# A partition order (t, part) for stages two and three, so that a chunk of z is one load and a chunk of u one store

## The chip, the cores and the metric

The kernel runs on one core of one Trainium2 chip. Its time is device microseconds of that core, from the launch to the end of the program. The time before is 1523.6 us, the median of 6 runs that lie between 1521.41 and 1527.71.

## What is computed

The reference has two blocks, one after the other. All of it is in float32.

```python
# attention block: a filter in the frequency domain; x is (8, 2496, 256)
X = np.fft.rfft(x, axis=1)
Y = X * (filt_r + 1j * filt_i)[None, :, :]
y = np.fft.irfft(Y, n=2496, axis=1)

# mixture of experts on the 8 * 2496 = 19968 rows; 8 experts, 256 -> 1024 -> 256
logits = x @ w_gate
expert_idx = np.argmax(logits, axis=1)
gate_w = softmax(logits)[arange, expert_idx]
# every row goes through its own expert alone
y = gate_w[:, None] * (np.maximum(x @ w1[expert_idx], 0.0) @ w2[expert_idx])
```

## The kernel before, in words

**The transform.** 2496 is 39 times 64, and the two factors have no common divisor, so the transform of a batch's 2496 rows is done as one of length 39 and one of length 64, with matrices and without twiddle factors in between. As the input is real, the transform of length 39 is kept as 20 frequencies f (`NF`) with two parts each, real and imaginary; the parts are called `c` in the code. The index in the transform of length 64 is `t`.

- Stage A (`stage_a`): the forward transform of length 39. Three values of `t` are handled by one matmul (117 rows in, 120 rows out). Its result `zo` is stored in the DRAM tensor `zd`, whose shape is (64 t, 40 part and f, 256 channels).
- Stage B (`stage_b`): the forward transform of length 64 for two f at a time, with the matrix `tbs` (128 by 128: 64 t times 2 parts), and then the product with the filter `ht` on VectorE, giving `ys`. Its input is a chunk of four f, read from `zd` by `load_z` into a buffer of the tag "in".
- Stage C (`stage_c`): the inverse transform of length 64 with `tcs`, giving `uo`, which is stored in the DRAM tensor `ud` (same shape as `zd`), a chunk of four f at a time.
- Stage D (`stage_d`): the inverse transform of length 39. It reads `ud` by `load_u` as 120 rows by four.

For the first batch there is no way through DRAM: `first_a`, `turn_z`, `first_c` and `turn_u` do the same in the core's memory, with transposes on TensorE from the tiles `zt` and `ut`.

**The partition order.** On the 128 partitions of a chunk of z, and of a chunk of u, the order before is (part, t): the 64 partitions below hold the real part of all t, those above the imaginary part. In `zd` and `ud` the two parts of one t are 20 rows of 256 channels apart. So `load_z` (lines 333 and 334) issues two transfers of 64 partitions, and `stage_c` (lines 392 and 393) two stores of 64 partitions. Each moves 64 pieces of 4 KB.

**Queues.** All direct transfers are issued by SyncE, in order. `move` puts off a store to the next turn of the planner, when `flush` issues it (so all stores have line 307). Transfers by index, which put the rows in the order of the experts (`scatter`, line 615) and the results in the order of the output (`result`, line 855), are issued by GpSimd. The framework gives SyncE's transfers 8 semaphores in turn: a transfer is issued when the one that was issued 8 places earlier has landed.

**Buffers.** Chunks of x, z and u that are read share 7 buffers of 512 KB (tag "in"). `zo` and `uo` share 4 buffers (tag "st"); a copy out of PSUM into one of them waits until its last store has landed.

**What sets the order.** At build time a planner writes down the order of TensorE, VectorE, ScalarE and SyncE. It keeps a model of time (`now`, and `lands` for when a transfer is thought to be there) and mixes the steps of stage A for batch k+1, B and C for batch k, D and the routing for batch k-1, and tiles of the experts' work, for which it asks rows (`rows_in`, tile `xg`) and weights (`weights`, tiles `w1t` and `w2t`). GpSimd's order is not written by hand but comes from the framework's scheduler. From about 950 us on only experts' work is left.

In the changed kernel the four orders written by the planner are the same, instruction by instruction, but that SyncE has one transfer where it had two, at 70 places. GpSimd's order differs at a few places between 155 and 729 us (times of the trace before): the sums of weights (`wsum`, lines 766 to 770) stand ahead of the sums of rows (`sums`, lines 754 to 758) or of one indirect store, where they stood behind or in between.

Of the kernel before, what the change touches and what calls it, by code (L numbers as in the profile page):

```python
# [10 lines left out]
F32 = mybir.dt.float32  # L11
# [8 lines left out]
P = 128  # L20
S = 2496
D = 256
# [5 lines left out]
N2 = 64  # L28
NF = (N1 + 1) // 2
# [6 lines left out]
DH = D // P  # L36
# [5 lines left out]
def token(q, t):  # L42
    return (q * N2 * pow(N2, -1, N1) + t * N1 * pow(N1, -1, N2)) % S


def coefficients():

    k = np.arange(S)
    of = np.zeros((N2, N1), int)
    of[k * pow(N1, -1, N2) % N2, k * pow(N2, -1, N1) % N1] = k  # L50
    return of[:, :NF]


def dft_tables():

    w = 2.0 * np.pi  # L60
    q = np.arange(N1)
    t = np.arange(N2)

    ta = np.zeros((NB, N1, NB, NS))
    td = np.zeros((NB, NS, NB, N1))
    for f in range(NF):
        ang = w * ((q * f) % N1) / N1
        for j in range(NB):
            ta[j, :, j, f] = np.cos(ang)
            td[j, f, j] = (2.0 if f else 1.0) / S * np.cos(ang)  # L70
            if f:
                ta[j, :, j, NF + f] = -np.sin(ang)
                td[j, NF + f, j] = -2.0 / S * np.sin(ang)

    ang = w * ((t[:, None] * t[None, :]) % N2) / N2
    c, sn = np.cos(ang), np.sin(ang)
    tb = np.block([[c, -sn], [sn, c]])
    tc = np.block([[c, sn], [-sn, c]])

    ids = np.zeros((NB, N1, NG))  # L80
    valid = np.zeros((NB, N1, NG))
    for j in range(NB):
        for i in range(len(range(j, N2, NB))):
            ids[j, :, i] = token(q, NB * i + j)
            valid[j, :, i] = 1.0


    sg = np.where(coefficients() <= S // 2, 1.0, -1.0)

    return {  # L90
        "ta": ta.reshape(TP, TK),
        "tb": tb,
        "tc": tc,
        "td": td.reshape(TK, TP),
        "sg": np.concatenate([sg[:, :NF // 2], sg[:, NF // 2:]]),
        "ids": ids.reshape(TP, NG),
        "valid": valid.reshape(TP, NG),
    }
# [22 lines left out]
def kernel(  # L121
# [16 lines left out]
    nc = tc.nc  # L138
    mm = nc.tensor.matmul
# [8 lines left out]
    for b in range(B):  # L148
        GROUPS.append([])
        for rows, most in WANT[b]:  # L150
            n = min(most, max(0, ((b + 1) * S - (N - left) - E * (rows - 1)) // rows))
# [8 lines left out]
    zd = [dram.tile([N2, NS, D], F32, tag=f"z{b % 2}", name="zd") for b in range(B)]  # L160
    ud = [dram.tile([N2, NS, D], F32, tag=f"u{b % 2}", name="ud") for b in range(B)]
# [6 lines left out]
    ident = perm.tile([P, P], F32, name="ident")  # L168
# [38 lines left out]
    pro = first.enter_context(tc.tile_pool(name="pro", bufs=2, side="right"))  # L207
# [7 lines left out]
    def bank():  # L215
        return ps.tile([P, 512], F32, tag="bank", name="bank")
# [5 lines left out]
    def either(n, on_vector, on_scalar):  # L222

        v = max(free["v"], now[0]) + 0.15 + n / 960
        s = max(free["s"], now[0]) + 0.16 + n / 1200
        if v <= s:
            free["v"] = v
            on_vector()
        else:
            free["s"] = s  # L230
            on_scalar()

    def evac(o, i, n):
        either(n, lambda: nc.vector.tensor_copy(o, i), lambda: nc.scalar.copy(out=o, in_=i))
# [6 lines left out]
    HP = P // 2  # L241
# [64 lines left out]
    def move(o, i):  # L306
        moves[1].append(lambda: nc.sync.dma_start(out=o, in_=i))

    def mark(key):
        moves[1].append(lambda: stored.add(key))  # L310
# [7 lines left out]
    def fin(key):  # L318
        ins[key] = sb.tile([P, 4, D], F32, tag="in", name="fin", bufs=NIN)
        return ins[key]  # L320

    def load_x(b, c):
        i0, n = CH[c]
        xt = fin(("x", b, c))

        for j in range(0, n, 2 if (b, c) == (0, 0) else n):
            m = 2 if (b, c) == (0, 0) else n
            nc.sync.dma_start(out=xt[:, j:j + m], in_=x[b, :, i0 + j:i0 + j + m, :])

    def load_z(b, c):  # L330
        f0, n = FH[c]
        zi = fin(("z", b, c))
        nc.sync.dma_start(out=zi[:HP, :n], in_=zd[b][:, f0:f0 + n, :])
        nc.sync.dma_start(out=zi[HP:, :n], in_=zd[b][:, NF + f0:NF + f0 + n, :])

    def load_u(b, c):
        i0, n = CH[c]
# [43 lines left out]
    def stage_c(b, f):  # L381
        ys = outs.pop(("y", b, f))
        j = f % 4
        if j == 0:
            outs["u", b] = sb.tile([P, 4, D], F32, tag="st", name="uo", bufs=4)
        uo = outs["u", b]
        p = bank()
        mm(p, lhsT=tcs, rhs=ys, start=True, stop=True)  # L388
        evac(uo[:, j:j + 2, :], p.rearrange("p (i d) -> p i d", i=2), 512)
        if j == 2:  # L390
            f0 = f - 2
            move(ud[b][:, f0:f0 + 4, :], uo[:HP])
            move(ud[b][:, NF + f0:NF + f0 + 4, :], uo[HP:])
        if f == NF - 2:
            mark(("c", b))

# [19 lines left out]
    zu = {}  # L416

    def first_a(c):
        i0, n = CH[c]
        xt = ins.pop(("x", 0, c))  # L420
        if c == 0:

            zu["z"] = pro.tile([P, DH, NF, 2, N2], F32, name="zt", bufs=1)
            zu["u"] = pro.tile([P, DH, N2, 2, NF], F32, name="ut", bufs=1)
        for j in range(0, n, 2):
            p = bank()[:, :4 * TK]
            for h in range(DH):
                for i in range(2):
                    mm(p[:, (2 * h + i) * TK:(2 * h + i + 1) * TK], lhsT=xt[:TP, j + i, h * P:(h + 1) * P], rhs=tas,
                       start=True, stop=True)  # L430
            t0 = NB * (i0 + j)
            m = min(2 * NB, N2 - t0)
            pv = p.rearrange("p (h t c f) -> p h c f t", h=DH, c=2, f=NF)[:, :, :, :, :m]
            zv = zu["z"].rearrange("p h f c t -> p h c f t")[:, :, :, :, t0:t0 + m]
            for h in range(DH):
                evac(zv[:, h], pv[:, h], 2 * TK)

    def turn_z(f):
        if f % 4 == 0:
            nc.scalar.copy(out=ht[HP:, f:f + 4], in_=ht[:HP, f:f + 4])  # L440
            free["s"] = max(free["s"], now[0]) + 1.1
        zi = outs["zi", f] = pro.tile([P, 2, D], F32, tag="zi", name="zi")
        p = bank().rearrange("p (i h d) -> p i h d", i=2, h=DH)
        for i in range(2):
            for h in range(DH):
                nc.tensor.transpose(p[:, i, h, :], zu["z"][:, h, f + i].rearrange("p c t -> p (c t)"), ident)
        evac(zi, p.rearrange("p i h d -> p i (h d)"), 2 * D)

    def first_c(f):
        ys = outs.pop(("y", 0, f))  # L450
        p = bank().rearrange("p (h i c t) -> p h i c t", h=DH, c=2, i=2)
        for i in range(2):
            for h in range(DH):
                mm(p[:, h, i].rearrange("p c t -> p (c t)"), lhsT=ys[:, i, h * P:(h + 1) * P],
                   rhs=tcs, start=True, stop=True)
        for h in range(DH):
            evac(zu["u"][:, h, :, :, f:f + 2], p[:, h].rearrange("p i c t -> p t c i"), D)

    def turn_u(c):
        i0, n = CH[c]  # L460
# [406 lines left out]
    def slot(k):  # L867

        steps, nch = [], len(CH)
        if k == 0:  # L870
            steps.append((0.4, load_rest, None, 0.0, None))
            for f in range(-2, NF + 2, 2):
                at = (f + 2) / (NF + 4)
                if 0 <= f < NF:
                    steps.append((at, lambda f=f: stage_b(k, f), None, 0.85, "b"))
                if f + 2 < NF:
                    steps.append((at + 0.01, lambda f=f: turn_z(f + 2), None, 0.44, "b"))
                if f >= 2:
                    steps.append((at + 0.02, lambda f=f: first_c(f - 2), None, 0.85, "b"))
        elif k < B:  # L880
            for f in range(0, NF + 4, 2):
                at = f / (NF + 4)
                if f < NF:
                    steps.append((at, lambda f=f: stage_b(k, f), ("z", k, f // 4) if f % 4 == 0 else None, 0.85, "b"))
                if f >= 4:
                    steps.append((at + 0.01, lambda f=f: stage_c(k, f - 4), None, 0.85, "b"))
# [173 lines left out]
    with tc.manual_schedule(  # L1060
# [17 lines left out]
        def other():  # L1078

            behind = set()  # L1080
            for n, f in enumerate(fs[:16]):
                if f[4] is None:
                    return 0
                if f[4] not in behind:
                    if ready(f) and not late_in(f):
                        return n
                    behind.add(f[4])
            return 0
# [3 lines left out]
        while fs or e:  # L1092
            f = fs[0] if fs else None
            asked = e and e[2] in when
            wait = f and (halted(f) or late_in(f))
            n = other() if wait else 0
# [5 lines left out]
            elif f and ready(fs[n]):  # L1102
                f = fs.pop(n)
# [52 lines left out]
```

## Time and profile before

| What | before |
|---|---|
| Median of 6 runs | 1523.6 us |
| The profiled execution: own time, span | 1527.33 us, 1525.6 us |
| TensorE matmul | 1467.9 us (96%) |
| VectorE | 754.8 us (49%) |
| ScalarE | 479.9 us (31%) |
| GpSimd | 697.0 us (46%) |
| SyncE's transfers: share of the 16 DMA engines | 54.0% |
| Loads of z; stores of u | 70 of 256 KB; 70 of 256 KB |
| Loads of x | 39 of 512 KB, 10 of 256 KB |

The median is 3.7 us below the profiled execution. A line of a wait reads: who waited, for whom, microseconds in total, how often, and the longest one. A line of the timeline reads: start and length in us, engine, line, operation, tile out and tile in, how many, and in brackets the idle time ahead of it with what ended it. "PEld" is TensorE's loading of weights, "SPq" is SyncE's queue. L362 is line 362 of the kernel.

### The profile page before, as it was taken

What the parts mean: (1) busy time and instruction counts of PE and PEld (TensorE: products, weight loads), DVE (VectorE), ACT (ScalarE), POOL (GpSimd) and SP (SyncE); (2) the same over time, 40 slices, a digit from 0 to 9 for tenths busy, and PEclk for the clock granted to TensorE, in tenths of its full rate; (3) what the DMA queues carried; (4) which work ended last, traced back from release to release, by engine and by line L of the source; (5) the groups of instructions that cost most, each with busy time, mean ns of one, the idle gap of its engine ahead of it and who ended that gap; (6) DMA issues with size and microseconds to landing.
All of it is one profiled execution on the core that took longest, in us unless ns stands there. A gap on an engine that the chain in (4) does not pass through costs nothing. (4 is left out here: it accounts for less than half of the span.)

```text
span 1525.6 us, 23882 instructions
## 1 busy us (share of the span) xinstructions
PE 1467.9 (96%) x7202; PEld 1159.8 (76%) x7202; DVE 754.8 (49%) x1676; ACT 479.9 (31%) x993; POOL 697.0 (46%) x910
## 2 busy tenths in 40 slices
PE   7998897899999999999999998999999999999998
PEld 6543554786677886788778876888888889999997
DVE  4577574424764657555764555566525343440000
ACT  3443442233333323222232223232222222224333
POOL 3243344323635564445644545774545556741111
PEclk9999998999999999999999999999999999999999
DMA  9669898878696649735683554545555443455661
GB/s 232 188 180 292 256 316 229 234 210 249 188 296 168 187 128 250 207 98 156 164 224 97 154 150 126 161 144 174 160 165 190 145 148 102 119 188 170 185 186 39
DMA packets 215173, 276.82 MB, mean 181 GB/s; under 512 B 124227, under 2 KB 162508, under 8 KB 215045
## 3 DMA queue, kind: packets, MB, share of 16 engines
q1 hardware_dynamic: 195925, 231.94, 54.0%
q0 software_dynamic: 19120, 43.33, 8.4%
q8 instruction: 61, 1.00, 0.3%
q14 instruction: 67, 0.55, 0.1%
HBM read 195.19 MB, written 80.64 MB: 181 GB/s over the span
## 5 line engine op out<-in xcount | busy, mean ns | idle before, releaser
L849 PE MATMUL bank<-w2t,hT 128*128 128x256 f32 x1984 | 444.3, 381 | 6.7 <-ACT hT L799 3.6
L795 DVE TENSOR_TENSOR hT<-bank,hT 128x512 f32<-128x512 f32 (+1 forms) x504 | 299.8, 627 | 295.8 <-PE bank L791 201.4
L849 PEld LDWEIGHTS bank<-w2t,hT 128*128 128x128 f32 x1984 | 377.4, 191 | 72.6 <-issue 13.6
L855 POOL DMA_INDIRECT out_dram<-ys,ng x161 | 161.4, 1003 | 471.4 <-DMA out_dram<-ys,ng 115.4
L799 ACT ACTIVATE hT<-hT 128x1024 f32<-128x1024 f32 (+1 forms) x144 | 132.3, 956 | 306.5 <-DVE hT L795 306.4
L615 POOL DMA_INDIRECT rows<-yo,row x176 | 177.3, 1007 | 73.3 <-issue 53.8
L854 ACT ACTIVATE ys<-bank,ng 128x256 f32<-128x256 f32 x137 | 65.0, 474 | 406.9 <-PE bank L849 309.9
L791 PE MATMUL bank<-xT,w1t 128*128 128x256 f32 (+1 forms) x864 | 191.6, 358 | 0.0
L791 PEld LDWEIGHTS bank<-xT,w1t 128*128 128x128 f32 x864 | 152.3, 191 | 24.9 <-issue 6.6
L791 PE MATMUL bank<-sums,wsum 128*128 128x256 f32 (+1 forms) x576 | 135.2, 357 | 0.0
L849 PE MATMUL bank<-w2s,hT 128*128 x592 | 132.6, 379 | 0.0
L748 DVE STREAM_TRANSPOSE xT<-xg 128x512 f32<-128x512 f32 (+2 forms) x126 | 57.5, 494 | 145.5 <-PE bank L832 125.6
L832 PE MATMUL bank<-xT,w1t 128*128 128x128 f32 (+1 forms) x864 | 124.3, 299 | 1.8 <-DVE xT L748 1.8
L832 PEld LDWEIGHTS bank<-xT,w1t 128*128 128x128 f32 x864 | 114.1, 191 | 12.9 <-issue 7.6
L849 PEld LDWEIGHTS bank<-w2s,hT 128*128 128x128 f32 x592 | 110.3, 190 | 13.8
L791 PEld LDWEIGHTS bank<-sums,wsum 128*128 128x128 f32 x576 | 101.0, 190 | 20.6 <-issue 9.7
L369 DVE TENSOR_TENSOR ys<-bank,ht 128x512 f32<-128x512 f32 x80 | 54.9, 687 | 74.7 <-PE bank L362 74.3
L348 PE MATMUL bank<-fin,tas 117*120 117x512 f32 x154 | 76.4, 616 | 9.0 <-DMA fin<-in_x_dram 8.1
L388 PE MATMUL bank<-ys,tcs 128*128 128x512 f32 x140 | 72.5, 601 | 8.0 <-DVE ys L378 5.4
L766 POOL TENSOR_TENSOR wsum<-w1t 128x256 f32<-128x256 f32 x72 | 53.3, 741 | 52.7 <-PE bank L791 52.0
L838 ACT ACTIVATE hT<-bank 128x128 f32<-128x128 f32 (+1 forms) x206 | 61.6, 299 | 48.4 <-PE bank L832 43.4
L362 PE MATMUL bank<-fin,tbs 128*128 128x512 f32 x140 | 72.0, 602 | 2.0 <-DMA fin<-zd 2.0
(143 smaller groups left out, 1616.9 us busy)
## 6 DMA issues: line engine op xcount, KB each, us to landing
w1t<-in_moe_w_dram SPq DMA_DIRECT2D x126, 512.0 KB
w2t<-in_moe_w_dram SPq DMA_DIRECT2D x68, 512.0 KB
fin<-in_x_dram SPq DMA_DIRECT2D x39, 512.0 KB
fin<-zd SPq DMA_DIRECT2D x70, 256.0 KB
ud<-uo SPq DMA_DIRECT2D x70, 256.0 KB
zd<-zo SPq DMA_DIRECT2D x35, 480.0 KB
fin<-ud SPq DMA_DIRECT2D x35, 480.0 KB
xg<-rows SPq DMA_DIRECT2D x112, 128.0 KB
```

Of the source, the lines that this page charges most:

```text
L348: mm(p[:TK, :], lhsT=tas, rhs=xt[:TP, j:j + 2, :], start=True, stop=True)
L362: mm(p, lhsT=tbs, rhs=zi[:, j:j + 2, :], start=True, stop=True)
L388: mm(p, lhsT=tcs, rhs=ys, start=True, stop=True)
L615: sc = nc.gpsimd.indirect_dma_start(out=rowsd, out_offset=bass.IndirectOffsetOnAxis(ap=at, axis=0), in_=what, in_offset=None,)
L791: mm(q[:, v], lhsT=left[:, v * P:(v + 1) * P], rhs=right, start=True, stop=True)
L795: nc.vector.tensor_tensor(o, q, a, op=ALU.add)
L799: nc.scalar.activation(o.rearrange("p v r c -> p v (r c)"), q.rearrange("p v r c -> p v (r c)"), AF.Relu)
L832: mm(p[:, :m], lhsT=w1t[2 * i + g][:, dh, fh, v * P:(v + 1) * P], rhs=xts[i][:, dh, :m], start=(dh == 0), stop=(dh == DH - 1))
L838: lambda: nc.scalar.activation(hT, p[:, :m], AF.Relu))
L849: mm(p[:, :D], lhsT=hs[i][k % 4 // 2][:, k // 4, k % 2, j * P:(j + 1) * P], rhs=w2, start=(k == 0), stop=(k == FT - 1))
L854: lambda: nc.scalar.activation(ys, p[:, :D], AF.Copy, scale=gate))
L855: nc.gpsimd.indirect_dma_start(out=out, out_offset=bass.IndirectOffsetOnAxis(ap=gis[i].bitcast(U32)[:, j, :1], axis=0), in_=ys, in_offset= ...
```

## The change

The rows of stage two's matrix and the columns of stage three's are put in the order (t, part), so that partition 2t + part of a chunk holds part `part` of t. In `zd` and `ud`, whose shapes stay, partition p then begins 20 rows of 256 channels after partition p-1. A chunk of z is one load, and a chunk of u one store, of 128 pieces of 4 KB over all 128 partitions. Columns of the matrix of stage two and rows of that of stage three, between which the filter stands, keep their order. In the first batch the tiles `zt` and the products of `first_c` take the new order; the copies out of PSUM into `zt` now write every second element of a run in memory.

```diff
-    tb = np.block([[c, -sn], [sn, c]])
-    tc = np.block([[c, sn], [-sn, c]])
+    tb = np.block([[c, -sn], [sn, c]]).reshape(2, N2, P).transpose(1, 0, 2).reshape(P, P)
+    tc = np.block([[c, sn], [-sn, c]]).reshape(P, 2, N2).transpose(0, 2, 1).reshape(P, P)
...
+    def by_part(ap):
+
+        return ap.rearrange("t (c f) d -> (t c) f d", c=2)
+
...
-        nc.sync.dma_start(out=zi[:HP, :n], in_=zd[b][:, f0:f0 + n, :])
-        nc.sync.dma_start(out=zi[HP:, :n], in_=zd[b][:, NF + f0:NF + f0 + n, :])
+        nc.sync.dma_start(out=zi[:, :n], in_=by_part(zd[b])[:, f0:f0 + n, :])
...
-            move(ud[b][:, f0:f0 + 4, :], uo[:HP])
-            move(ud[b][:, NF + f0:NF + f0 + 4, :], uo[HP:])
+            move(by_part(ud[b])[:, f0:f0 + 4, :], uo)
...
-            zu["z"] = pro.tile([P, DH, NF, 2, N2], F32, name="zt", bufs=1)
+            zu["z"] = pro.tile([P, DH, NF, N2, 2], F32, name="zt", bufs=1)
...
-            zv = zu["z"].rearrange("p h f c t -> p h c f t")[:, :, :, :, t0:t0 + m]
+            zv = zu["z"].rearrange("p h f t c -> p h c f t")[:, :, :, :, t0:t0 + m]
...
-                nc.tensor.transpose(p[:, i, h, :], zu["z"][:, h, f + i].rearrange("p c t -> p (c t)"), ident)
+                nc.tensor.transpose(p[:, i, h, :], zu["z"][:, h, f + i].rearrange("p t c -> p (t c)"), ident)
...
-        p = bank().rearrange("p (h i c t) -> p h i c t", h=DH, c=2, i=2)
+        p = bank().rearrange("p (h i t c) -> p h i t c", h=DH, c=2, i=2)
...
-                mm(p[:, h, i].rearrange("p c t -> p (c t)"), lhsT=ys[:, i, h * P:(h + 1) * P],
+                mm(p[:, h, i].rearrange("p t c -> p (t c)"), lhsT=ys[:, i, h * P:(h + 1) * P],
...
-            evac(zu["u"][:, h, :, :, f:f + 2], p[:, h].rearrange("p i c t -> p t c i"), D)
+            evac(zu["u"][:, h, :, :, f:f + 2], p[:, h].rearrange("p i t c -> p t c i"), D)
```

## The prediction

> **What bounds the kernel now.** First the page's busy lines: TensorE is at work 1467.9 us of a span of 1525.6, so all its idle time is 57.7 us, and no change to transfers can bring more than that and what a lowered clock costs.
>
> ```profile
> span 1525.6 us, 23882 instructions
> PE 1467.9 (96%) x7202; PEld 1159.8 (76%) x7202; DVE 754.8 (49%) x1676; ACT 479.9 (31%) x993; POOL 697.0 (46%) x910
> DMA  9669898878696649735683554545555443455661
> ```
>
> Second, the busy time by stretches of 50 us, to see where the idle time lies. Columns: stretch, its length, busy us of PE, PEld, DVE, ACT, POOL, granted clock, busy share of the DMA engines, GB/s.
>
> ```profile
> 100.00:150.00 50.00, 43.12 (x120) 18.36 (x119) 40.75 (x101) 18.38 (x41) 19.65 (x25) 0.97 0.89 272
> 150.00:200.00 50.00, 44.95 (x212) 27.38 (x211) 25.12 (x61) 20.06 (x48) 20.73 (x25) 1.00 0.90 263
> 200.00:250.00 50.00, 41.59 (x174) 19.80 (x173) 33.76 (x107) 21.75 (x49) 25.07 (x35) 0.94 0.96 294
> 250.00:300.00 50.00, 43.88 (x171) 34.48 (x170) 22.88 (x59) 10.10 (x23) 13.52 (x17) 0.89 0.83 231
> 300.00:350.00 50.00, 50.00 (x211) 39.02 (x211) 15.47 (x45) 15.77 (x35) 13.78 (x17) 1.00 0.77 218
> ```
>
> From 100 to 300 us TensorE idles 26.5 us and the DMA engines are 83 to 96% busy; from 300 us on TensorE is full nearly everywhere. So the change, which touches transfers of z (58 to 770 us) and u (90 to 900 us), can pay or cost only where transfers bound, and that is 100 to 260 us. Third, TensorE's waits and its timeline there:
>
> ```profile
> PE bank L348 <- DMA fin<-in_x_dram: 8.1, 3, 6.6
> PE bank L362 <- DMA fin<-zd: 2.0, 1, 2.0
> PE bank L407 <- DMA fin<-ud: 1.7, 3, 1.3
> ```
>
> ```profile
> 239.77 1.90 PE L348 MATMUL bank<-fin,tas 117*120 117x512 f32 x4
> 248.22 3.45 PE L348 MATMUL bank<-fin,tas 117*120 117x512 f32 x4 [6.55 <-DMA fin<-in_x_dram]
> 253.69 2.79 PE L362 MATMUL bank<-fin,tbs 128*128 128x512 f32 x4 [2.01 <-DMA fin<-zd]
> ```
>
> The one large wait is for a chunk of x at 241.67 us (6.55), then one for z (2.01). The same four matmuls took 1.90 us before the wait and 3.45 after it: the clock stood at half. The records of the granted clock have it at 0.5 in 244.43–251.26, 254.67–258.08 and 278.56–285.39 here. Fourth, SyncE's queue:
>
> ```profile
> 240.33 0.41 SPq L328 DMA_DIRECT2D fin<-in_x_dram  x1
> 240.83 1.59 SPq L307 DMA_DIRECT2D zd<-zo  x2
> 248.83 0.47 SPq L333 DMA_DIRECT2D fin<-zd  x1
> 249.36 0.59 SPq L334 DMA_DIRECT2D fin<-zd  x1
> 250.04 0.54 SPq L333 DMA_DIRECT2D fin<-zd  x1
> 250.63 0.59 SPq L334 DMA_DIRECT2D fin<-zd  x1
> 251.32 1.18 SPq L307 DMA_DIRECT2D ud<-uo  x2
> ```
>
> The x chunk, issued at 240.33, landed at 248.09 behind two loads of w1t and one of w2t; the z loads wait for stores of zo that landed at 248.69; behind them stand the stores of uo, for whose buffers VectorE waits 18.4 us in one piece (until 256.94).
>
> **The prices.** From the trace's landing times I take the steps from one landing to the next where the queue was backed up. Medians (means in brackets): first half of z 1.14 (1.15), second half 1.03 (1.04), so 2.17 a chunk; a half of u 0.69 (0.97), so 1.38 (1.94) a chunk; a whole chunk of x, 128 pieces of 4 KB, 1.86 (1.93); w2s, same size, 1.49; a store of zo, 480 KB in pieces of 1 KB, 1.38 (1.50); a load of u, 480 KB in such pieces, 2.38. Issuing one transfer costs SyncE 0.47 to 0.60 us.
>
> **The change, part by part.**
>
> *A chunk of z as one load.* Nearest row is the x chunk: it has the same piece, partitions and nearly the same step in DRAM (22 KB for 20). So 2.17 − 1.86 = 0.31 us less a chunk. Bounds: 0.68 less (w2s), 0.21 more (the load of u). Ten chunks are issued between 100 and 241 us, and the engines are backed up through most of that: 3.1 us (−2.1 to 6.8).
>
> The row tells of 256 KB in 1.03 to 1.14 us, some 230 to 255 GB/s, for a half, and 282 for a whole x. The Trainium skill (SBUF — State Buffer, Door 1: The DMA port swizzle) says that partitions 0 to 63 reach only 8 of 16 ports, about 218 GB/s against 436. By it a whole chunk would take some 1.2 us, an estimate, ten chunks would save 9.7 us instead of 3.1, and the sum below would be some 12. The x row, which covers all partitions and still takes 1.86, speaks against that much, and the halves of u, at 0.69 us or 380 GB/s, break the rule for stores.
>
> *A chunk of u as one store.* Nearest row is the store of zo over 120 partitions; scaled to 512 KB 1.47 (mean 1.60). Against 1.38 (1.94) that is 0.09 more by medians, 0.34 less by means. I take 0.1 less, between the two; eleven chunks up to 241 us make 1.1 us. Bounds: 0.56 less each, from the halves' mean 1.94 to their median 1.38; 1.16 more each, from 1.38 to the load of u, 2.38 × 512/480 = 2.54: −12.8 to 6.2.
>
> *Seventy issues fewer.* SyncE runs in order, and a transfer waits for the landing of the one 8 places ahead. One place in place of two lets SyncE run further ahead, but with the engines 96% busy what counts is when the bytes are through: nothing, except where SyncE starts afresh after a wait. At 248.83 that is one issue for the z that TensorE waits for, 0.6 us, and two for the stores of uo. Nobody waits longer by it: both halves were already needed for any reader, and both stores for any reuse of the buffer.
>
> *What eats of it.* The chain of transfers is tied at places to VectorE and ScalarE: in 100 to 300 us SyncE waits for zo 3.9 and 2.2, yt 3.9, lg 3.3. Those don't move by themselves; I take off 1.2 us (0 to 4).
>
> *The clock.* TensorE worked at half rate in 248.22–251.26, 254.67–258.08 and 279.16–285.39, 12.7 us, of which half, 6.3, is lost. With less idle ahead some of it goes; I take a third, 2.1 (0 to 6.3; a new lowered stretch of 3.4 or 6.8 us would cost 1.7 to 3.4).
>
> *The first batch.* Copies into zt write with a step of two: 11 on ScalarE (363 ns), 11 on VectorE (408). The nearest strided writes, into ut, take 424 ns on ScalarE where the plain 40x256 copy takes 366, and 426 to 418 on VectorE. So 0 to 0.06 us a copy; they hide behind TensorE's matmuls (ScalarE waited 12.6 us for them), and only the last stands free: 0. Copies into ut may gain or lose 0.06 each, 14 on ScalarE, −0.8 to 0.8: 0.
>
> *GpSimd's order.* Sums of weights move ahead of sums of rows, four of 0.73 us, so either may end 2.9 us later. After 55 us TensorE has no listed wait for GpSimd, and where sums ended at 406.9 and 724.3 it used them, with the next experts' tile, from 418.0 and 737.2 on, 11 us later or more: 0.
>
> Sum: 3.1 + 1.1 + 0.6 − 1.2 + 2.1 = 5.7, say 6 us. After 300 us TensorE is full and the gain is carried to the end. From the execution's own 1527.3 that gives 1521.3; it lies 3.7 above the median 1523.6, so the median goes to 1517.6.
>
> **Rivals.**
>
> *Given back or never got (same).* TensorE still idles at 885.06 (2.61), 918.82 (2.24) and 936.23 (2.72), for VectorE and ScalarE, the last behind the stores of rows by index. If those are paced by GpSimd and not by TensorE, an earlier arrival only makes them longer, up to 6 us. For it: the releasers aren't transfers that the change touches. Against: 600 us lie between, and GpSimd itself waits for results of TensorE. Then, or if x's landing stays where its weight loads put it, the time is 1522 to 1524.
>
> *Slower: the store of u over 128 partitions.* If it drains at the load of u's pace, 2.54 us instead of 1.38, eleven chunks cost 12.8 us in the stretch with no spare transfer time; less 3.1 for z, 0.6 for issues, and with the clock not gained, it is some 9 us, 1533. It decides from about 0.35 us more a chunk on, where it eats z's gain. For it: the halves of u are the fastest transfers here per byte, so merging can hardly quicken them. Against: zo's store, smaller pieces, is nearly as fast.
>
> *Nothing changes in speed.* If two halves in a row cost the engines the same as a whole, z gains 0, and 0.6 to 1.1 us are left: 1522.5.
>
> **How the numbers follow.** About 0.3%, 4.6 us, is what a measurement of this kernel can tell. Forecast (6 us, with its own range from 1509 to 1519): 0.52. Given back, never got or no change in speed together: 0.26. Slower by the store, or by a clock lowered at a new place: 0.22. With the best bounds, 6.8 + 6.2 + 0.6 + 6.3, the time would be 1504, but not all together; 8 times in 10 I take 1508 to 1528: the upper end takes in half of the slower case; the lower is the best of z and of the clock together (6.8 + 1.1 + 0.6 + 6.3 = 14.8).
>
> **What would show it.** Steps: z's landing step near 1.86 a chunk; u's near 1.3 to 1.5; 35 issues each; the DMA share of 200–250 us below 0.96; the wait for x at 241.67 down from 6.55 to 3 or less, or reached earlier; fewer stretches of clock 0.5. Wrong if u's step is over 1.8, if that wait stays, or if idle time at 885–939 us grows by what was gained.

## The result, and the profile after

The median after is 1516.9 us (1513.2 to 1524.6) against 1523.4 us for the kernel before on the same chip: a ratio of 0.9959, with a 95% interval from 0.995 to 0.9968. That is 6.5 us less; 1517.6 had been forecast. (Ratios and their intervals are the recorded ones here and below; they differ a little from the quotient of the two medians, by 0.3% at the most.) The profiled execution took 1513.61 us, 3.3 below its median, where that of before lay 3.7 above (1527.33). So the two traces are 13.7 us apart, twice what the medians are, and half of what they show is chance of the single execution.

The head of the page of the kernel after, with the queue of SyncE's transfers:

```profile
span 1511.9 us, 23787 instructions
PE 1464.7 (97%) x7202; PEld 1160.0 (77%) x7202; DVE 755.5 (50%) x1676; ACT 480.1 (32%) x993; POOL 696.9 (46%) x910
DMA  9659898696694559534764464546555533456661
q1 hardware_dynamic: 194805, 231.94, 52.7%
```

TensorE's idle time, span less busy, went from 57.7 to 47.2 us: 10.5 less. Its busy time fell by 3.2 us for the same 7202 matmuls. Together that is the 13.7. The 3.2 is the clock: ahead of the last 20 us, the records of the granted clock have it at half for 27.3 us before and 20.5 after, and half of that difference is 3.4. SyncE's queue took 52.7% of 1511.9 us, 797, against 54.0% of 1525.6, 824: 27 us less for the same bytes, 0.77 us for each pair of a chunk of z and a chunk of u. The transfers themselves became cheaper, not only their number smaller: the 1120 packets that fell away have 4 bytes each, and all packets of that size together took 8.7 us before and 7.7 after by the same measure.

The busy time by stretches, kernel after; columns as before (stretch, length, busy us of PE, PEld, DVE, ACT, POOL, granted clock, DMA share, GB/s):

```profile
100.00:150.00 50.00, 44.87 (x131) 19.96 (x131) 41.99 (x102) 21.16 (x47) 19.21 (x25) 0.97 0.91 298
150.00:200.00 50.00, 45.88 (x207) 27.44 (x206) 26.67 (x69) 18.87 (x46) 21.67 (x26) 1.00 0.90 290
200.00:250.00 50.00, 44.39 (x178) 22.04 (x177) 34.53 (x103) 21.68 (x49) 26.76 (x37) 0.90 0.92 298
250.00:300.00 50.00, 47.02 (x218) 40.43 (x217) 26.32 (x85) 12.38 (x29) 19.14 (x23) 1.00 0.75 213
300.00:350.00 50.00, 50.00 (x207) 37.10 (x206) 14.70 (x24) 17.89 (x39) 6.47 (x10) 1.00 0.90 259
```

From 100 to 300 us TensorE is busy for 182.2 us in place of 173.5. The DMA engines are as busy as before up to 200 us, at 26 to 27 GB/s more: bytes go through faster. From 200 to 300 the share falls, 0.96 to 0.92 and 0.83 to 0.75, and from 300 to 350 it rises, 0.77 to 0.90: the kernel after is ahead, so other transfers fall into these stretches. The 300–350 row is also a counter-check: TensorE was full there already and has nothing to win.

TensorE's waits for x behind the first batch, and its timeline at the place of the old wait of 6.55 us, kernel after:

```profile
PE bank L351 <- DMA fin<-in_x_dram: 1.8, 1, 1.8
```

```profile
238.81 3.08 PE L351 MATMUL bank<-fin,tas 117*120 117x512 f32 x4 [1.82 <-DMA fin<-in_x_dram]
243.63 3.78 PE L365 MATMUL bank<-fin,tbs 128*128 128x512 f32 x4 [1.73 <-DMA fin<-zd]
```

The wait for x is now 1.82 us and ends 9.4 us earlier; that for z is 1.73 in place of 2.01. The four matmuls behind it still run at half clock (3.08 us; they take 1.90 at full): a short wait did not save this stretch, though the one at 278 us is gone. SyncE's queue there, kernel after:

```profile
231.39 0.37 SPq L332 DMA_DIRECT2D fin<-in_x_dram  x1
231.85 0.87 SPq L307 DMA_DIRECT2D zd<-zo  x2
239.68 0.82 SPq L337 DMA_DIRECT2D fin<-zd  x2
240.59 1.15 SPq L307 DMA_DIRECT2D ud<-uo  x1
```

The chunk of x is issued at 231.39 instead of 240.33: SyncE came 8.9 us earlier to the same place of its order. Behind the wait for the stores of zo stand two loads of z and one store where there were four loads and two stores.

I followed the same TensorE instruction through both traces. The kernel after is 0.6 us ahead at 110 us, 4.7 at 165, 4.2 at 210, 9.4 at 248, 13.8 at 290, then 13.8 at 400, 13.0 at 700, 13.7 at 870, 12.0 at 900, 14.1 at 940 and 13.7 at the end. The gain is made from 120 to 290 us, as forecast, and is carried to the end. The late waits, in the timeline of the kernel after, that were to swallow it by one rival:

```profile
874.00 1.44 PE L498 MATMUL lt<-yt,wg 128*32 128x234 f32 x8 [2.60 <-DVE yt L234]
909.03 1.22 PE L484 MATMUL bank<-ident,yo 117*128 117x117 f32 x8 [2.25 <-DVE yo L234]
924.84 5.45 PE L851 MATMUL bank<-w2t,hT 128*128 128x256 f32 x24 [0.64 <-ACT yo L234]
```

They were 2.61, 2.24 and 2.72: two are the same, and the third is shorter.

### The profile page after: what moved, and what is told of

The parts are those of the page before. It is cut to its first block, busy times and chain, and to the rows that moved or that the text cites. A ratio compares the mean times of both kernels' runs of the same rounds, so it can differ in the third digit from the quotient of the medians.

```text
span 1511.9 us, 23787 instructions
## 1 busy us (share of the span) xinstructions
PE 1464.7 (97%) x7202; PEld 1160.0 (77%) x7202; DVE 755.5 (50%) x1676; ACT 480.1 (32%) x993; POOL 696.9 (46%) x910
## 3 DMA queue, kind: packets, MB, share of 16 engines
q1 hardware_dynamic: 194805, 231.94, 52.7%
## 5 line engine op out<-in xcount | busy, mean ns | idle before, releaser
L851 PEld LDWEIGHTS bank<-w2s,hT 128*128 128x128 f32 x592 | 110.3, 190 | 13.8
```

Of the source, the lines that this page charges most:

```text
L851: mm(p[:, :D], lhsT=hs[i][k % 4 // 2][:, k // 4, k % 2, j * P:(j + 1) * P], rhs=w2, start=(k == 0), stop=(k == FT - 1))
```

## The experiments

**The theory.** A transfer over all 128 partitions goes through the DMA engines faster than two over 64 one after the other; where transfers bound the kernel, the steps from one landing to the next are what it gains. (A transfer over all partitions also has 128 pieces in place of 64; the runs do not part the two, and "width" below means both.) **Rivals:** the order (t, part) itself does it; or that SyncE issues 70 transfers fewer, and takes 70 turns fewer of its eight semaphores; or only one of the two merges counts.

The runs below were made on three other chips, and each is compared with the kernel before on its own chip. On two of them the kernel before takes 1561.7 and 1556.8 us, on the third 1524.7. "Step" is the median (mean) distance from one landing to the next where SyncE's queue was backed up, of a half or of a whole chunk. In the kernel before the two halves of z take 1.14 and 1.03 us, together 2.17 (2.19), a half of u 0.69 (0.97). In the kernel after a chunk of z takes 1.58 (1.65), one of u 1.49 (1.58). A step is not the time of a transfer by itself: transfers that follow each other can overlap. "Queue time" is the share of SyncE's queue on the page times the span, as above: it tells what the bytes cost the DMA engines, whoever waits for them.

**The load of z alone** (stage three and its stores as before):

```diff
-    tc = np.block([[c, sn], [-sn, c]]).reshape(P, 2, N2).transpose(0, 2, 1).reshape(P, P)
+    tc = np.block([[c, sn], [-sn, c]])
...
-            move(by_part(ud[b])[:, f0:f0 + 4, :], uo)
+            move(ud[b][:, f0:f0 + 4, :], uo[:HP])
+            move(ud[b][:, NF + f0:NF + f0 + 4, :], uo[HP:])
```

> Only the loads of z are merged (stage two's rows in order (t, part)); the stores of u stay two of 64 partitions. My theory, that a chunk over 128 partitions drains faster and that the chain of transfers to the x chunk at 240 us is shortened by the sum over the chunks: z saves 0.59 us a chunk (2.17 to 1.58) and u 0.36 (mean 1.94 to 1.58), ten and eleven chunks, so z has about 60% of the gain: ratio to before about 0.9975, 1519.6 us; the wait for x at 241.67 (6.55) falls to about 3. Rival, only the stores of u pay (their buffers hold VectorE up for 18 us): ratio 1.000. Rival, one edit alone removes the whole wait: 0.996.

Measured: 1555.4 against 1561.7 us, ratio 0.9961 (0.994 to 0.9982). The step of z is 1.29 (1.45), that of a half of u 0.79 (0.92). TensorE's waits, z alone:

```profile
PE bank L365 <- DMA fin<-zd: 4.3, 1, 4.3
PE bank L351 <- DMA fin<-in_x_dram: 1.1, 1, 1.1
```

The wait for x is small here too, smaller than the 3 us expected; what is late next is z. The gain is above the expected 0.25%, and near the rival's 0.4%, but it has to be held against the halves below, which gain 0.25% without any merge. SyncE's queue on the page, z alone:

```profile
q1 hardware_dynamic: 195365, 231.94, 53.2%
```

Of a span of 1556.8 us that is 828 us of queue time.

**The store of u alone** (stage two and its loads as before):

```diff
-    tb = np.block([[c, -sn], [sn, c]]).reshape(2, N2, P).transpose(1, 0, 2).reshape(P, P)
+    tb = np.block([[c, -sn], [sn, c]])
...
-        nc.sync.dma_start(out=zi[:, :n], in_=by_part(zd[b])[:, f0:f0 + n, :])
+        nc.sync.dma_start(out=zi[:HP, :n], in_=zd[b][:, f0:f0 + n, :])
+        nc.sync.dma_start(out=zi[HP:, :n], in_=zd[b][:, NF + f0:NF + f0 + n, :])
```

> Only the stores of u are merged (stage three's columns in order (t, part)); z stays two loads of 64 partitions. My theory: u has about 40% of the gain, ratio about 0.9985, 1521 us; u's landing step is 1.5 to 1.6 us, z's stays at 1.1 and 1.0. Rival, only the stores pay: 0.996. Rival, only the loads pay: 1.000.

Measured: 1557.7 us, ratio 0.9966 (0.9946 to 0.9986). The step of u is 1.25 (1.27), below the 1.5 to 1.6 expected; those of z are 1.10 and 1.05 as before. The gain, 0.34%, was expected at 0.15%; here too the halves are the measure. SyncE's queue on the page, u alone:

```profile
q1 hardware_dynamic: 195365, 231.94, 53.5%
```

Of 1555.7 us that is 832.

**The order (t, part), but two transfers of 64 partitions each**:

```diff
-        nc.sync.dma_start(out=zi[:, :n], in_=by_part(zd[b])[:, f0:f0 + n, :])
+        for r in (slice(0, HP), slice(HP, P)):
+            nc.sync.dma_start(out=zi[r, :n], in_=by_part(zd[b])[r, f0:f0 + n, :])
...
-            move(by_part(ud[b])[:, f0:f0 + 4, :], uo)
+            for r in (slice(0, HP), slice(HP, P)):
+                move(by_part(ud[b])[r, f0:f0 + 4, :], uo[r])
```

> The order (t, part) of the changed kernel is kept in both matrices, in zt and in DRAM, but each chunk goes in two transfers of 64 partitions, below and above. My theory: the order alone brings nothing, ratio 1.000 (0.998 to 1.002), halves of z again at 1.0 to 1.15 us. Rival, the step of 20 KB in place of 40 KB in DRAM is what pays: ratio 0.996. If the strided copies into zt cost anything, it shows here as slower.

Measured: 1557.8 us, ratio 0.9975 (0.9956 to 0.9994). A half of z takes 1.04 (1.03), a half of u 0.66 (0.69). TensorE's waits, halves:

```profile
PE bank L352 <- DMA fin<-in_x_dram: 5.8, 1, 5.8
PE bank L836 <- DMA w1t<-in_moe_w_dram: 2.1, 1, 2.1
```

The long wait for x is back. SyncE's queue, halves:

```profile
q1 hardware_dynamic: 195925, 231.94, 54.0%
```

Of 1559.5 us that is 842. On another chip the same kernel:

> e3 once more: order (t, part), two transfers of 64 partitions each. e3 gave 0.9975, its interval just short of 1. My theory, that the order alone brings nothing: 1.000 within 0.2%. Rival, that the step of 20 KB or the different order on GpSimd brings a part: 0.9975 again.

Measured: 1553.1 against 1556.8 us, ratio 0.998 (0.9964 to 0.9997); steps 1.04 (0.97) and 0.66 (0.78); 54.0% of 1551.5 us, 838. Both intervals end just below 1, which leaves 0.2% to the order, or to the comparison. So the kernel before was set against itself:

> The kernel before itself, as a control for the two runs of the halves (0.9975 and 0.998, both with an interval that ends just below 1) and for a profile of it on the chip of the other runs. If a comparison here can be trusted to 0.2%, the ratio is 1.000 with an interval that holds 1, and the halves' 0.2% is real. If the ratio comes out at 0.998 or 1.002 with an interval that leaves 1 out, the halves' gain can't be told from none. In its profile the theory (width of a transfer sets its time) expects 2.0 to 2.2 us for the two landing steps of a chunk of z, as in the halves (1.04 each), and TensorE's wait for x near 240 us at 5 to 6.5 us.

Measured, on the third of these chips: 1523.5 against 1524.7 us, ratio 0.9991 (0.9974 to 1.0008). In its profile the steps of the two halves of z are 1.15 (1.11) and 1.03 (1.04) and the longest wait for x is 5.0 us, as expected. A difference of 0.1 to 0.2% is at the edge of what can be told; the halves' 0.2% can't be told from nothing. Of the order there is left that, or 0.4% by the ends of the two intervals (0.9956 and 0.9964), where the merge gains 1.1 to 1.2% on the same chips. On the first chip, where the whole gain is 0.41%, the halves were not run.

**The changed kernel itself, on the three chips.**

> The changed kernel once more, beside the three others on the same chip, for the comparison and for a second profile. Ratio 0.996 as before. My theory of the profile: the two profiled executions stood 13.7 us apart but the medians 6.5, because single executions differ by how long the clock stands at half; in this profile the shift against before's profile at 239 us is again 4 to 5 us, and at 290 us it is 8 to 14 us. Rival, the profile of after was typical and the medians differ for another reason: 13 to 14 again at 290.

Measured: 1544.2 against 1561.7 us, ratio 0.9886 (0.9858 to 0.9914), so the 0.996 expected was missed; steps of z 1.34 (1.54), of u 1.45 (1.60). Against the halves' trace on the same chip the same instruction of TensorE comes 5.6 us earlier at 239 us and 9.0 at 290, near what was expected (4 to 5 and 8 to 14). Against before's trace on the first chip the shifts are −2.8 and 3.7, but there the chip differs too. SyncE's queue, changed kernel on the chip of the two parts and of the first halves:

```profile
q1 hardware_dynamic: 194805, 231.94, 52.7%
```

> The changed kernel once more, for comparison on the chip of this call. Ratio to before between 0.989 and 0.996, what the two chips so far gave.

Measured: 1534.0 against 1556.8 us, ratio 0.988 (0.9837 to 0.9922), just outside the range expected; steps 1.56 (1.61) and 1.28 (1.50); queue time 52.4% of 1533.1 us, 803.

> The changed kernel once more beside the two others, for the comparison on one chip: 0.987 to 0.993 of the kernel before if the chip is one of those on which that takes about 1557 us; 0.995 to 0.997 if it is one on which that takes about 1523 us. With the control beside it, the two figures tell whether the gain depends on the chip's own time.

Measured: 1513.7 against 1524.7 us, ratio 0.9914 (0.9888 to 0.994); steps 1.32 (1.59) and 1.51 (1.61). Here the expectation (0.995 to 0.997 where before takes about 1523 us) missed: the gain is 0.9%. Against the trace of the kernel before on this chip the kernel after is 6.4 us ahead at 290 us and 5.6 at the end.

On the first of these chips all four can be set side by side:

| Kernel | queue time | time | against halves |
|---|---|---|---|
| halves, order (t, part) | 842 us | 1557.8 us | |
| load of z alone | 828 | 1555.4 | −14 of queue time, −2.4 of time |
| store of u alone | 832 | 1557.7 | −10, −0.2 |
| changed kernel | 814 | 1544.2 | −28, −13.7 |

For the DMA engines the parts fit together: 14 and 10 make 24, and both together are 28 (a share is rounded to 0.1%, 1.6 us). That is 0.40 us for each of 35 chunks of z and 0.28 for each of u. But each figure is from one trace: from two halves to one transfer the queue time falls by 28 us here, by 27 on the first chip, by 35 and 21 on the other two. So the queue time speaks for both merges, and which of them brings more can't be told. The steps show it for the load alone: two halves of z take 2.1 to 2.2 us, one load 1.32 to 1.58 by the medians of the changed kernel. For the store they show nothing: two halves in the new order take 1.32 (1.38 to 1.56), one store 1.25 to 1.51 (1.27 to 1.60).

The time at the end does not follow in proportion: each part alone brings it next to nothing over the halves, both together 13.7 us, with intervals of some 3 us to either side. The place of the gain explains it in part. At 290 us, where the stretch that transfers bound is over, the trace of the load alone is 6.3 us ahead of the halves', that of the store alone 3.9, that of the changed kernel 9.0: there the parts do add up. At the end they are 2.7, 3.9 and 15.7 ahead, and between the halves and the changed kernel the differences behind 290 us are made at places like the wait for the routing near 408 us (2.10 us in the halves, 1.28 in the changed kernel) and in stretches of lowered clock, not at waits for z or x. These are single traces, and what decides there is open.

**Two transfers, each over 128 partitions** (two of the four f each, so pieces of 2 KB; as many issues as before):

```diff
-        nc.sync.dma_start(out=zi[:, :n], in_=by_part(zd[b])[:, f0:f0 + n, :])
+        for j in (0, 2):
+            nc.sync.dma_start(out=zi[:, j:j + 2], in_=by_part(zd[b])[:, f0 + j:f0 + j + 2, :])
...
-            move(by_part(ud[b])[:, f0:f0 + 4, :], uo)
+            for k in (0, 2):
+                move(by_part(ud[b])[:, f0 + k:f0 + k + 2, :], uo[:, k:k + 2])
```

> Order (t, part) as in the changed kernel, but each chunk goes in two transfers again, each over all 128 partitions with two of the four f (128 pieces of 2 KB). So the count of issues and of turns of the eight semaphores is that of before, the width that of after. My theory, width pays: the step of a z chunk stays near 1.6 us for both, and the time is that of the changed kernel, at most 0.1% above. Rival, fewer issues and turns pay: the time is that of two halves (e3, 0.9975 of before). Where the pieces of 2 KB drain worse than those of 4 KB, it shows in the step.

Measured: 1544.5 us, ratio 0.9918 (0.9886 to 0.995), on the chip where the halves have 0.998 and the changed kernel 0.988. A transfer of 256 KB over 128 partitions has a step of 0.66 (0.93) for z, where one over 64 partitions has 1.04; for u it has 0.64 (0.71), hardly below the 0.66 (0.78) of one over 64. Two wide loads of z make 1.32 (1.86), below the 1.6 expected by the median, above it by the mean; the time was expected within 0.1% of the changed kernel's. The rows of the loads by tile, halves on that chip first, then two wide ones (count, then shortest, median and longest time on SyncE, first and last start):

```profile
L338 SPq DMA_DIRECT2D fin<-zd x70: 4/587/1950, 55.1 to 786.3; - x70
```

```profile
L338 SPq DMA_DIRECT2D fin<-zd x70: 319/430/1592, 54.9 to 785.2; - x70
```

As many transfers of the same 256 KB in both, and still 8.6 us between the times, and 23 us of queue time (52.5% of 1551.9 us, 815, against 838): width pays by itself. The changed kernel on this chip is another 10.5 us faster by the medians, with 12 us less of queue time, but the intervals of the two overlap (0.9886 to 0.995 and 0.9837 to 0.9922). So whether pieces of 4 KB in place of 2, or fewer issues, bring anything besides is not shown.

**Seventy small transfers put back** (64 bytes behind each merged transfer, so that SyncE issues as many and uses up as many turns as before):

```diff
+    def tick():
+        nc.sync.dma_start(out=sb.tile([1, 16], F32, tag="tick", name="tick", bufs=8), in_=tb[0:1, :16])
...
         nc.sync.dma_start(out=zi[:, :n], in_=by_part(zd[b])[:, f0:f0 + n, :])
+        tick()
...
             move(by_part(ud[b])[:, f0:f0 + 4, :], uo)
+            moves[1].append(tick)
```

> The changed kernel, with a transfer of 64 bytes put behind each merged one, into a small tile that nothing reads: 70 more issues on SyncE, 70 more turns of the eight semaphores, no bytes to speak of. My theory, width pays: the time of the changed kernel plus at most 1 us. Rival, fewer turns pay, SyncE runs further ahead: the time of two halves (e3).

Measured: 1540.9 us, ratio 0.9892 (0.9868 to 0.9916), beside 0.988 (0.9837 to 0.9922) for the changed kernel without them; queue time 807 us against 803. The medians are 6.9 us apart, the ratios 0.1%, and the intervals overlap nearly whole: seventy more issues and turns cost at most a few us, and it can't be told from nothing.

**Loads of w1 one step later until 250 us**, an attempt at a better version:

```diff
-        h - used[what] < ((3 if h < 2 * SHORT else 8) if what == "w1" else ...
+        h - used[what] < ((2 if now[0] < 250.0 else 3 if h < 2 * SHORT else 8) if what == "w1" else ...
```

> The changed kernel with one more edit: until 250 us the loads of w1 run two steps ahead of their use instead of three, so that fewer of them stand ahead of the chunks of x and z in the queue. Theory one (transfers bound up to 290 us, and what stands in the queue ahead of x decides the wait): the wait for x near 240 us, 1.9 to 3.2 us in the changed kernel, falls below 1, and the time is 1 to 3 us below the changed kernel's on the same chip, 0.1 to 0.2%. Theory two (the bytes are the bound, and their order matters nothing): the wait moves to a chunk of z or to w1 itself, and the time is that of the changed kernel, within 0.3%. Theory three: w1 arrives late and the planner's order shifts, 3 to 10 us slower than the changed kernel.

Measured: 1516.1 us, ratio 0.9934 (0.991 to 0.9958); the changed kernel beside it has 1513.7. TensorE's waits, w1 later first, then the changed kernel on the same chip:

```profile
PE bank L851 <- ACT hT L801: 7.3, 1, 7.3
PE bank L365 <- DMA fin<-zd: 3.0, 1, 3.0
PE bank L351 <- DMA fin<-in_x_dram: 0.4, 2, 0.2
```

```profile
PE bank L851 <- ACT hT L801: 3.6, 1, 3.6
PE bank L351 <- DMA fin<-in_x_dram: 2.4, 1, 2.4
PE bank L365 <- DMA fin<-zd: 1.6, 1, 1.6
```

The wait for x goes from 2.4 to 0.4, that for z from 1.6 to 3.0, and the next layer's wait for ScalarE from 3.6 to 7.3. Putting x ahead only moves the wait, as the second theory of its expectation has it: the bytes bound here and not their order. The time can't be told from the changed kernel's. No version beat the changed kernel.

## Why the prediction was right, point by point

**Where.** Right on the first chip, for which it was made. The gain is made from 120 to 290 us and carried to the end; the signs that the prediction named came: 35 issues of z and of u in place of 70, DMA share of 200–250 us from 0.96 to 0.92, the wait for x from 6.55 at 241.67 to 1.82 at 236.99. In the kernel after, the rows by tile of the load of z and the store of u:

```profile
L337 SPq DMA_DIRECT2D fin<-zd x35: 320/352/2190, 58.3 to 757.3; - x35
L307 SPq DMA_DIRECT2D ud<-uo x35: 319/338/1267, 89.8 to 886.9; - x35
```

On the third of the other chips it is the same (6.4 us at 290 us, 5.6 at the end). On the first two of them it is not: the changed kernel is 9.0 and 8.5 us ahead of the halves at 290 us, but 15.7 and 18.4 at the end. So 6.7 and 9.9 us of it were made behind 290 us, where the prediction saw nothing to gain.

**"A chunk of z as one load": mis-sized.** The chunk of x was taken as the nearest row, 1.86 us; z as one load takes 1.58 (1.65) in the profile after and 1.29 to 1.76 (1.45 to 1.79) in the others. So 0.59 us a chunk less (0.54 by means) instead of 0.31, and some 0.40 by the queue time: 4.0 to 5.9 us for ten chunks instead of 3.1, inside the bound of 6.8. x itself is unchanged (1.81 after). Why x, with the same pieces and partitions, is slower than z wasn't tried.

The Trainium skill (SBUF — State Buffer, Door 1: The DMA port swizzle) has 64 partitions reach half the ports. For loads the runs lean to it: 256 KB into 64 partitions have a step of 1.04 us, into 128 partitions 0.66 (0.93 by the mean), and a whole chunk comes to 1.29–1.76, between the row's 1.86 and the 1.2 estimated from the page. For stores they speak against it: 256 KB from 64 partitions have a step of 0.66 us, 397 GB/s, far above the page's 218. The prediction took this for a breach of the rule, but it is none for certain: the two halves of a chunk lie in different halves of the partitions and may be on their way together, and both together, 512 KB in 1.32 us, stay below the page's 436. The Trainium skill's page DMA: Bandwidth & Descriptors (Rules for kernel authors) says without a number that two transfers to disjoint partition halves serialize and should be one. The merge's 0.4 to 1.2% agrees with the advice.

**"A chunk of u as one store": its size is not known.** The step after was forecast well, 1.47 (1.60), and came to 1.49 (1.58). But the saving was put between the medians (0.09 more) and the means (0.34 less), at 0.1. Eleven chunks times a step is a sum, and a sum follows the mean: 1.94 − 1.58 = 0.36 us, 4.0 in place of 1.1. The queue time, which is a sum by nature, says some 0.28, or 3.1. But steps in other traces scatter: the mean of two halves in the new order is 1.38 to 1.56, and against one store's 1.27 to 1.60 nothing is left. So by the steps not even the sign is known; for a gain speak the queue time and the 3.9 us at 290 us of the store alone, one trace each.

**"Seventy issues fewer", 0.6 us.** Not contradicted and not shown: what the small transfers cost can't be told from nothing.

**"The clock", 2.1 us: mis-sized.** Between 238 and 286 us the records have the clock at half for 17.1 us in both traces of the kernel before, and for 10.2 in both of the changed kernel on chips where it takes 1514 to 1517 us. Half of the 6.8 between them is 3.4.

**"What eats of it", −1.2 us; the first batch and GpSimd, 0.** Copies into `zt`, which now write every second element, went from 363 to 376 ns on ScalarE and from 408 to 409 on VectorE; ahead of 56 us the trace after is 0.7 us late, and that is made up by 70. No new wait for GpSimd stands among TensorE's. The 1.2 can't be told apart.

**The sum.** With what was measured it is 9.9 by the queue time (4.0 + 3.1 + 0.6 − 1.2 + 3.4) and 12.2 by the mean steps (5.4 and 4.0 in front), which fits the 13.7 between the traces and not the 6.5 between the medians. So that the median came within 0.7 us of the forecast is in part luck: the terms were too small by half for the pair of profiled executions, and that pair lay 7 us further apart than the medians. The second pair of traces on a chip of the same speed is 5.6 us apart, near the forecast, with 21 us less of queue time (835 and 814), so the same merge gave 13.8 us at 290 us in one pair and 6.4 in the other. What decides between the two in a single execution, the runs don't show.

**The rivals.** "Given back": refuted by the shift that stays at 12.0 to 14.1 us and by the late waits (5.6 to 6.2 of 6.4 us stay behind 700 us in the second pair). "Slower by the store of u": refuted, its step is 1.25 to 1.51, not 2.54, in every trace with nothing put between. "Nothing changes in speed": refuted by the queue time, and by the halves, which gain 0.2% (0.4 at most by their intervals) where the merge gains 1.1 to 1.2%.

## What to carry to other kernels

If a tile is moved as two transfers of 64 partitions because a matrix puts real above imaginary parts, interleave them by reordering the matrix's rows and columns; one transfer over 128 partitions was cheaper here, clearly so for the loads, for the stores by the queue time alone. Price a queue of transfers by the mean step between landings times the count, from more than one trace and only in the stretch where the DMA engines are full, and hold it against the queue's share of the span; the median hides the slow ones. And set the terms against the medians of many executions: here two traces alone would have told twice the gain.

## What the runs showed of the hardware that was not expected

The gain depends on the chip or the occasion: 0.41% on the first (interval 0.32 to 0.5%), 0.86% on one where the kernel before takes the same time, 1.14 and 1.2% on two where it takes 33 to 38 us more. On those two the idle time and the lowered clock are more. The head of the page for the halves on the second chip, then for the kernel before on the third:

```profile
span 1551.5 us, 23886 instructions
PE 1482.9 (96%) x7202; PEld 1165.9 (75%) x7202; DVE 749.2 (48%) x1676; ACT 479.2 (31%) x993; POOL 697.7 (45%) x910
```

```profile
span 1523.5 us, 23882 instructions
PE 1468.8 (96%) x7202; PEld 1161.8 (76%) x7202; DVE 754.8 (50%) x1676; ACT 479.4 (31%) x993; POOL 695.0 (46%) x910
```

Of the 28 us between them 13.9 are idle time of TensorE (68.6 and 54.7) and 14.1 longer matmuls for the same count. The records of the clock have it at half for 47.8 us in the first, ahead of the last 20, and 30.7 in the second; half of that difference, 8.5 us, would be its part of the 14.1. In the first VectorE has waits that nothing in the profile ended ("issue"), ten of them with 8.7 us in all; the second has none:

```profile
DVE hT L799 <- issue: 6.6, 6, 2.7
DVE ys L373 <- issue: 1.1, 3, 0.7
DVE zo L234 <- issue: 1.0, 1, 1.0
```

At some places the changed kernel loses less (TensorE waits 0.29 us at 394 us for a tile of the routing for which the halves wait 2.64). What delays the engines on those chips, and why the gain on two like chips is 0.4 and 0.9%, stays open.
